# A longer warm-up and a new order of all instructions in a kernel of a long convolution and a gated MLP

## The chip, the cores and the metric

The kernel runs on one core of a Trainium2 chip. The metric is the device time of one execution in microseconds; lower is better. A core has five engines that run side by side, each through its own list of instructions in order: TensorE (PE, matrix multiplication), VectorE (DVE), ScalarE (ACT), GpSimd (POOL) and SyncE (SP). SP and ACT here also issue DMA transfers, each on a queue of its own. Engines wait for each other by semaphores only.

## What is computed

The reference, cut to what matters (x is A_q; S = 2048 positions, 512 channels, 1792 hidden units):

```python
xn = layernorm(x)
# long convolution
k_shift = sum(k_pad[:, t:t + S] * shift_k[:, 3 - t] for t in range(4))
kv = k_shift * v
y = irfft(rfft(kv, 2 * S) * rfft(ssm_k, 2 * S))[:S] + kv * ssm_D
s = xn * y
# gated MLP
h = gelu(xn @ w_gate) * (xn @ w_up)
g = silu(h @ w_down)
out = x + s * g
```

All inputs are bfloat16.

## The kernel before

The MLP is done in four quarters q of 512 positions. For a quarter, `ln` (L824) makes the statistics of its four tiles of x on VectorE (L827, L828, L835), a power on GpSimd (L836) and the normalized tile XN on VectorE or ScalarE (L845, L846). `xn_transpose` (L855) turns XN into xnT, for the first two quarters with TensorE transposes (L867) and an evacuation out of PSUM (L610 on ScalarE, L613 on VectorE), for the last two with a DMA transpose on SP's queue (L859). `unit` (L1130) is one of 14 blocks of 128 hidden units: four matmuls with w_gate and four with w_up (both recorded at L619), a GELU on ScalarE (L1149, L1158) and a product on VectorE (L1151, L1161). The first two blocks of the first quarter are done in halves of 256 columns. `down` (L1164) multiplies with w_down. w_gate and w_up come in four chunks (wg0 to wg3, wu0 to wu3: two blocks, then four each), w_down in two (wd0, wd1).

The convolution is a Fourier transform in two stages. The filter ssm_k (tiles Hn, loads h0 to h3) is transposed on TensorE (`h_transpose`, L883, matmuls at L891, evacuated to HTr) and goes through the first stage (`stage1`, L916): matmuls of HTr with the Fourier matrices F0 and F1, an evacuation by ScalarE or VectorE, and a store of 512 KB to the scratch tensor ZH, which ScalarE issues on its own DMA queue. `kshift` (L961) makes the shifted product of k and v on VectorE, whose first stage (L925) is stored to ZK by SP. The second stages read BH and BK back (L1001, in tiles of 32 by 32), the spectra are multiplied, transformed back, stored to ZI, read as BI, and the last stage (L1231) gives y.

At the very front TensorE has nothing to do until x arrives. `warm_up` (L677) fills that time with N_WARM matmuls of zeros with 512 columns into a bank that nobody reads.

All loads are issued by SP in the order of ORDER (L26), one list item after the other. The order of all other instructions is written out by hand, in SEQ (L27): a list of task numbers, in which a task is a few instructions on one engine (a "b" behind the number picks the second engine that it may run on). `Sched.run` (L345) walks through the list, emits the tasks to their engines in that order, and picks the buffer and the PSUM bank of each by a plan of times. LAND (L52) gives the plan's landing times of the loads, in ns; TAKEN (L301) is what a store on ScalarE's queue adds there to a load still in flight that stands ahead of it in the list. These times enter the program only through the choice of buffers; the order of each engine is SEQ's.

Of the kernel before, what the change touches and what calls it, by code (L numbers as in the profile page):

```python
# [21 lines left out]
NB = 2  # L22
LN_EPS = 1e-5
TURN = 8192
N_WARM = 12
ORDER = "x00 h0 x01 w0 D0 h1 w1 x1 h2 h3 s0 k0 w2 k1 k2 w3 d0 d1 k3 v2 v3 v0 v1 x2 x3"  # L26
SEQ = (  # L27
    "0 16 17 18 19 20 21 22 23 24 25 26 27 28 29 30 31 32 33 34 35 36 37 38 39 40 41 42 43 44 45 2 10 7 3 11 67 8 4 5 6 1 68 76 65 77 66 9 73 12 78 "
    "87 74 75 71 72 48 86 82 83 49 91 90 341 69 70 79 80 84 349 81 135 13 50 343 350 51 89 93 342 88 92b 137 351 352 14 52 54 344 53 55 345 346 353 "
    "134 355 15 354 356 365 347 348 124 125 431 425 426 427 104 429 129 105 369 361 367 371 56 428 366 58b 432 430 363 130 368 60 62 362 364 64 61 63 "  # L30
    "370 372 57 433 59 109 111 110 357 138 136 112 131 132 139 140 141 359 358 360 385 133 381 383 106 107 382 377 113 434 435 142 143 436 439b 384 "
    "126 144 379 378 380 146 437b 127 387 128 386 388 373 440b 119 397 443 441 374 375 376 389 447 147 148 438b 444 448 399 401 403 445 120 398 400 "
    "402 391 442 393 121 395 122 99 390 394 404 149 150 114 396 392 446 453 100 116 461 151 152 115 117 118 145 101 154 463 96 462 102 123 497 455 "
    "108 153 103 499 415 155 94 416 95 97 464 498 156 98 417 418 419 465 467 217 157 500 158 466 405 218 219 485 178 487 468 225 220 226 227 228 159 "
    "406 162 420 46 407 408 213 160 457 170 409 421 214 47 454 163 215 216 459 221 222 223 224 422 486 161 85 164 410 233 488 411 165 473 234 235 475 "
    "171 173 412 413 456 236 229 166 172 230 231 167 168 458 460 501 449 503 451 169 502 504 232 241 474 414 477 423 424 242 243 476 237 622 624 478 "
    "469 618 489 479 480 244 625 525 238 239 471 179 180 619 620 621 623 626 181 470 450 452 491 481 483 472 529 174 175 176 627 628 490 492 493 629 "
    "632 630 482 633 484 494 631b 495 496 240 183 182 184 531 505 527 510 506 245 526 185 532 528 530 533 186 246 706 258 188 177 282 634 534 247 249 "
    "520 507 515 248 250 259 187 261b 535 269 260b 198 516 511 536 537b 508 509 540b 538b 539b 541 517 252 518 519 189 190 521 191 192 251 262 512 "
    "513 514 522 523 524 193 253 256 639 263 254 655 657 635 637 283 284 285b 641 640 656 709 270 272 647 651 255 271b 658 642 264 265 267b 636 638 "  # L40
    "648 293 330 306 649 650 199 550 652 653 273 274 200 654 201 268 586 257 588 574 552 576 276 275 194 195 196 575 587 589 202 203 551 553 577 687 "
    "689 277 280b 278 197 590 592 546 294 279 548 286 287 296 295 208 547 549 570 572 591 593 307 309 308 297 298 281 266 688 690 578 288 289 291 290 "
    "566 568 580 299 571 567 573 569 204 205 206 300 310 317 659 542 660 543 712 661 662 544 545 311 209 210 562 211 212 594 596 579 581 301 302 304b "
    "564 303 207 563 595 597 305 318 320 565 671 319b 558 321 323 560 554 556 312 673 313 559 561 555 315 582 314 331 332 333 322 584 663 316 583 557 "
    "643 645 292 672 324 325 598 585 326 327 683 328 329 599 334 335 685 336 674 684 339 340 667 337b 338 686 665 664 600 601 703 666 608 669 675 677 "
    "644 609 646 694 602 695 603 610 611 679 668 681 604 670 696 713 710 612 680 682 676 678 605 613 606 714 766 711 764 698 697 699 719b 700 607 715 "
    "716 717 768 614 732 701 615 616 702 721b 725 739 723 724 617 718 720 770 733 691 692 693 707 771 704 705 722 760 761 734 726 740 746 769 767 727 "
    "765 735 747 741 753 728 742 708 762 763 729 748 736 737 738 730 731 749 754 755 743 744 745 756 750 751 752 757 758 759 "
)
NF_BANKS = 4  # L50
ISSUE = 470.0
LAND = {"x0_0": 3000, "h0": 6000, "x0_1": 7200, "wg0": 8300, "wu0": 9300, "D": 6500, "h1": 10700, "wg1": 12900, "wu1": 14600, "x1": 16000, "h2": 17400, "h3": 18700, "sk": 20000, "kh1": 21100, "kh113": 21300, "kz": 14000, "k0": 22700, "wg2": 24400, "wu2": 26100, "k1": 27600, "k2": 29100, "wg3": 30600, "wu3": 32100, "wd0": 34600, "wd1": 37200, "k3": 38500, "v2": 39800, "v3": 41100, "v0": 42400, "v1": 43700}  # L52
W_XT, W_SW, W_BK, W_BH, W_ZI, W_BI, W_ZK, W_MI, W_G1 = 1665000, 600000, 555000, 703000, 333000, 640000, 490000, 740000, 222000
NC_PAIRS = 4
SMALL = 1.15 * 262144
# [24 lines left out]
class Trk:  # L80
# [29 lines left out]
    def res(self, name, ap):  # L110
        t = ap.tensor
        tn = type(t).__name__
        if tn.startswith("SB"):
            key = "SB"
            addr = self.nc.lookup_mloc(t).addr
        else:
            assert tn.startswith("PS")
            key = "PS:" + t.name
            addr = 0
        esz = mybir.dt.size(ap.dtype)  # L120
        pairs = [list(q) for q in ap.ap]
        pst, pn = pairs[0]
        pstart = ap.offset // pst if pst else 0
        inner = ap.offset - pstart * pst
        hi = sum(st * (n - 1) for st, n in pairs[1:])
        r = Res(name, key, pstart, pstart + pn, addr + inner * esz, addr + (inner + hi + 1) * esz)
        lst = self.res_by_key.setdefault(key, [])
        for o in lst:
            if o.plo < r.phi and r.plo < o.phi and o.blo < r.bhi and r.blo < o.bhi:
                o.ovl.append(r)  # L130
                r.ovl.append(o)
        lst.append(r)
        return r
# [156 lines left out]
class Sched:  # L290
# [7 lines left out]
    SHARE_BW = 300.0  # L298
    FIRST = {"loads": 300.0, "SP": 37000.0}
    DRAIN, DRAIN2 = 121.0, 97.0  # L300
    SHARED, WAIT, TAKEN = 46000.0, 3300.0, 1400.0  # L301

    def __init__(self):
        self.tasks = []
# [91 lines left out]
def build_kernel(nc, A_q, A_k, A_v, A_shift_k, A_ssm_k, A_ssm_D, B_w_gate, B_w_up, B_w_down, out):  # L396
    with ExitStack() as es0:
# [11 lines left out]
        def new(name, shape, dt):  # L409
            h = at(name, shape, dt, place["at"])  # L410
            place["at"] += size(shape, dt)
            return h
# [4 lines left out]
        X = new("X", [128, NT, DM], BF16)  # L417
# [80 lines left out]
        S = Sched()  # L498
        res = trk.res

        def dsem(name):
            return DSem(nc.alloc_semaphore(name), name)
# [4 lines left out]
        def bank(b):  # L507
            return PSALL[:, 512 * b.slot:512 * (b.slot + 1)]
# [4 lines left out]
        def R_bank(b):  # L513
            return [R_ps[b.slot // 2][b.slot % 2]]
        R_X = [res(f"X{t}", X[:, t, :]) for t in range(NT)]
# [75 lines left out]
        def dma(eng, out_ap, in_ap, sem, r, w):  # L591
            trk.dma(eng, lambda e: e.dma_start(out=out_ap, in_=in_ap), sem, r=r, w=w)
# [3 lines left out]
        def load(name, out_ap, in_ap, w_res, w_buf, nbytes, ring="SP", r=(), rb=()):  # L596
            sem = dsem("d_" + name)
            last_load[0] = S.add([("loads", ISSUE)], lambda e: dma(ring, out_ap, in_ap, sem, r, w_res), r=rb, w=w_buf, nbytes=nbytes, land=float(LAND[name]))

# [18 lines left out]
        def mm(h, o, l, r, st, sp):  # L618
            return h.matmul(o, lhsT=l, rhs=r, start=st, stop=sp)  # L619
# [3 lines left out]
        bX = [[B(f"X{q}_{t}") for t in range(4)] for q in range(NQ)]  # L623
# [47 lines left out]
        bwarm = B("warm")  # L671
# [4 lines left out]
        warm = B("pswarm", pF)  # L676

        def warm_up(e):
            for i in range(N_WARM):
                trk.op("PE", lambda h: mm(h, bank(warm), ZERO[:, 0:128], ZERO, True, True), r=[R_zero], w=R_bank(warm), accum=True)  # L680

        t_warm = S.add([("PE", 10 * 390.0 + (N_WARM - 10) * 220.0)], warm_up, r=[bwarm], w=[warm])
        bcq, bck, bid32 = B("cq"), B("ck"), B("id32")
        S.add([("POOL", 420.0)], lambda e: pool_q(), w=[bcq])
        S.add([("POOL", 1000.0)], lambda e: pool_k(), w=[bck])
# [65 lines left out]
        x_dr = A_q[0].rearrange("(p t) d -> p t d", t=NT)  # L751
# [24 lines left out]
            x_late.append(S.add([("SP", ISSUE)], lambda e: dma(e, args[0], args[1], sem, [], args[2]), w=args[3], nbytes=480000, after=last_load))  # L776

        def load_x0(t):
            ts = slice(2 * t, 2 * t + 2)
            load(f"x0_{t}", X[:, ts, :], x_dr[:, ts, :], R_X[ts], bX[0][ts], 262144)  # L780

        def load_w(i, rings=("SP", "SP")):
            f0, n = FC[i]
# [117 lines left out]
        for k in range(KD):  # L901
# [4 lines left out]
                    r=[bHD, *[bHTr[k][0] for k in range(KD)]], w=[bFold], rr=[R_D, *R_HTr[0]], ww=R_HTr[0])  # L906
# [328 lines left out]
        for j in range(8):  # L1235
            p = p_y[j]
            ts = slice(2 * j, 2 * j + 2)
# [16 lines left out]
        for j in range(6):  # L1254
# [7 lines left out]
                  r=[b2], w=[B(f"out{j}")], nbytes=262144)  # L1262
# [55 lines left out]
```

## Time and profile before

| what | value |
| --- | --- |
| median of 3 runs | 194.51 us (194.4 to 194.63) |
| the profiled execution | 196.12 us, of it 194.3 us span |
| TensorE busy | 188.0 us, 1514 matmuls |
| VectorE busy | 158.2 us, 231 instructions |
| ScalarE busy | 137.7 us, 186 instructions |
| HBM | 27.39 MB read, 14.68 MB written |
| mean granted clock of TensorE | 0.991 |

The span runs from the program's first to its last instruction. "Busy" is the time in which an engine has at least one instruction of its own in flight; matmuls overlap, and their ends are modelled. A group of instructions is named by its line and by what it writes and reads (psall is the whole of PSUM). The chain of waits is followed back from the last instruction: at each step to what released it, or to the instruction before it on its engine. The granted clock is the share of its full clock at which TensorE was allowed to run.

### The profile page before, as it was taken

What the parts mean: (1) busy time and instruction counts of PE and PEld (TensorE: products, weight loads), DVE (VectorE), ACT (ScalarE), POOL (GpSimd) and SP (SyncE); (2) the same over time, 40 slices, a digit from 0 to 9 for tenths busy, and PEclk for the clock granted to TensorE, in tenths of its full rate; (3) what the DMA queues carried; (4) which work ended last, traced back from release to release, by engine and by line L of the source; (5) the groups of instructions that cost most, each with busy time, mean ns of one, the idle gap of its engine ahead of it and who ended that gap; (6) DMA issues with size and microseconds to landing.
All of it is one profiled execution on the core that took longest, in us unless ns stands there. A gap on an engine that the chain in (4) does not pass through costs nothing.

```text
span 194.3 us, 3771 instructions
## 1 busy us (share of the span) xinstructions
PE 188.0 (97%) x1514; PEld 84.7 (44%) x1514; DVE 158.2 (81%) x231; ACT 137.7 (71%) x186; POOL 14.3 (7%) x32
## 2 busy tenths in 40 slices
PE   7699999999999999999999999999999999999993
PEld 2485644544434333343434433343444354444452
DVE  4878799989999798977897898899788762279784
ACT  2787899698687889895969487878767643263452
POOL 5311360000000000023000000000000000000000
PEclk9789999999999999999999999999999999999999
DMA  5999999993967997589999997841353344866056
GB/s 154 353 384 346 364 365 370 411 401 117 363 204 246 303 270 200 199 287 320 273 285 180 335 369 266 281 140 54 126 201 108 110 163 131 305 216 216 22 200 213
DMA packets 36423, 47.86 MB, mean 246 GB/s; under 512 B 7347, under 2 KB 26039, under 8 KB 36406
## 3 DMA queue, kind: packets, MB, share of 16 engines
q1 hardware_dynamic: 29878, 39.23, 62.6%
q10 hardware_dynamic: 6528, 8.39, 12.2%
q8 instruction: 12, 0.20, 0.4%
q14 instruction: 5, 0.04, 0.1%
HBM read 27.39 MB, written 14.68 MB: 217 GB/s over the span
## 4 chain that ended last, share of the span: by engine, by line
PE 94%; DMA 2%; DVE 2%; ACT 0%; issue 0%
PE psall L619 80%; PE psall L1001 6%; PE psall L891 2%; PE psall L925 2%; DMA X<-in_A_q_dram 2%; PE psall L1231 2%; PE psall L867 1%; DVE stats L827 1%; DVE G L1196 0%; DVE G L1195 0%; ACT G L1193 0%; DVE XN L846 0%; DVE mv L835 0%; DVE mv L828 0%; DVE C L701 0%
## 5 line engine op out<-in xcount | busy, mean ns | idle before, releaser
L619 PE MATMUL psall<-xnT,Wg 128*128 128x512 bf16 (+1 forms) x232 | 56.3, 376 | 0.0
L619 PE MATMUL psall<-xnT,Wu 128*128 128x512 bf16 (+1 forms) x232 | 55.7, 372 | 0.0
L619 PE MATMUL psall<-Wd,HT 128*128 128x512 bf16 (+2 forms) x238 | 52.3, 367 | 0.0
L1161 DVE TENSOR_TENSOR HT<-psall,GE 128x512 bf16<-128x512 f32 x54 | 36.5, 687 | 18.8 <-PE psall L619 17.5
L1158 ACT ACTIVATE GE<-psall 128x512 bf16<-128x512 f32 x54 | 31.3, 600 | 9.1 <-PE psall L619 8.1
L619 PEld LDWEIGHTS psall<-Wd,HT 128*128 128x128 bf16 x238 | 21.9, 98 | 27.1 <-issue 3.8
L619 PEld LDWEIGHTS psall<-xnT,Wg 128*128 128x128 bf16 x232 | 22.0, 99 | 25.9 <-issue 2.2
L619 PEld LDWEIGHTS psall<-xnT,Wu 128*128 128x128 bf16 x232 | 21.4, 98 | 25.7 <-issue 2.6
L610 ACT ACTIVATE BO<-psall 128x1024 bf16<-128x1024 f32 x18 | 17.9, 1022 | 12.0 <-PE psall L1231 6.5
L1104 DVE TENSOR_TENSOR HSW<-KB,HSW 128x2048 bf16<-128x2048 bf16 x16 | 19.1, 1218 | 1.8 <-ACT KB L610 1.7
L610 ACT ACTIVATE HSW<-psall 128x1024 bf16<-128x1024 f32 x16 | 15.5, 1026 | 2.8 <-PE psall L1001 2.8
L1185 ACT ACTIVATE G<-psall 128x512 bf16<-128x512 f32 x12 | 7.2, 596 | 12.4 <-PE psall L619 12.4
L984 DVE TENSOR_TENSOR KAC<-KAC,KTM 128x2048 bf16<-128x2048 bf16 x12 | 14.6, 1220 | 0.2
L982 DVE TENSOR_TENSOR KTM<-KK,SKB 128x2048 bf16<-128x2048 bf16 x12 | 14.6, 1219 | 0.1
L610 ACT ACTIVATE KB<-psall 128x1024 bf16<-128x1024 f32 x11 | 10.8, 1022 | 4.3 <-PE psall L1001 4.3
L610 ACT ACTIVATE AST<-psall 128x1024 bf16<-128x1024 f32 x12 | 12.2, 1020 | 1.1 <-PE psall L925 0.7
L836 POOL TENSOR_TENSOR mv<-mv,NHALF 128x1 f32<-128x1 f32 (+1 forms) x7 | 6.8, 970 | 69.2 <-DVE mv L835 69.2
L827 DVE BATCH_NORM_STATS2 stats<-X 128x6 f32<-128x512 bf16 x16 | 10.4, 678 | 1.7 <-DMA X<-in_A_q_dram 1.7
L1104 DVE TENSOR_TENSOR KB<-KB,HSW 128x2048 bf16<-128x2048 bf16 x8 | 9.7, 1218 | 0.0
L610 ACT ACTIVATE XN<-psall 128x1024 bf16<-128x1024 f32 x8 | 8.1, 1020 | 1.5 <-PE psall L619 1.3
L619 PE MATMUL psall<-HTr,F 128*128 128x512 bf16 x32 | 8.7, 379 | 0.0
L613 DVE CAST BO<-psall 128x1024 bf16<-128x1024 f32 x5 | 6.1, 1223 | 2.6 <-PE psall L1001 2.6
(83 smaller groups left out, 162.3 us busy)
## 6 DMA issues: line engine op xcount, KB each, us to landing
BH<-ZH SPq DMA_DIRECT2D x8, 512.0 KB, 5.0
HSW<-HSW SPq DMA_DIRECT2D x16, 256.0 KB, 2.8
BK<-ZK SPq DMA_DIRECT2D x8, 512.0 KB, 6.0
ZI<-BO ACTq DMA_DIRECT2D x16, 256.0 KB, 3.4
BI<-ZI SPq DMA_DIRECT2D x8, 512.0 KB, 4.6
ZK<-AST SPq DMA_DIRECT2D x6, 512.0 KB, 3.2
Hn<-in_A_ssm_k_dram SPq DMA_DIRECT2D x4, 512.0 KB, 7.4
KK<-in_A_k_dram SPq DMA_DIRECT2D x4, 512.0 KB, 12.0
```

The lines of the kernel that those rows point to most:

```text
L610: return h.activation(o, i, ACTF.Copy, scale=scale)
L613: return h.tensor_copy(o, i)
L619: return h.matmul(o, lhsT=l, rhs=r, start=st, stop=sp)
L827: t_stats[t] = op([("DVE", 670.0)], lambda e, h, t=t: h.bn_stats(stats[:, t, :], X[:, t, :]), r=[bX[q][t % 4]], w=[bst[t]], rr=[R_X[t]], w ...
L836: t_pw = op([("POOL", 850.0 if q else 600.0)], lambda e, hd, ts=ts, n=n: hd.tensor_tensor(mv[:, ts, 3:4], mv[:, ts, 2:3], NHALF[:, 0:n, :] ...
L982: op([("DVE", dur)], lambda e, h, j=j, m=m: h.tensor_tensor(KTM[:, m.slot, :, :], kk(j), sk(j), ALU.mult), r=need + [bSKB[j], a], w=[m], r ...
L984: op([("DVE", dur)], lambda e, h, m=m: h.tensor_tensor(KAC[:, a.slot, :, :], KAC[:, a.slot, :, :], KTM[:, m.slot, :, :], ALU.add), r=[m], ...
L1001: trk.op("PE", lambda h: h.matmul(ps(s, i)[b, :], lhsT=wt(col)[a, :], rhs=data(col)[a, :], start=n < 16, stop=n >= len(todo) - 16, tile_po ...
L1104: return hd.tensor_tensor(pair(KB, *(2 * DM * z for z in slots())) if to else x, k, x, ALU.mult)
L1158: op([("ACT", act(512))], lambda e, h: h.activation(GE[:, g.slot, :], bank(pg), ACTF.Gelu_apprx_tanh), r=[pg], w=[g], rr=lambda: R_bank(pg ...
L1161: op([("DVE", dve(512, 1))], lambda e, h: h.tensor_tensor(HT[:, q % 2, m, :], bank(pu), GE[:, g.slot, :], ALU.mult), r=[pu, g], w=[bHT[q][m]],
L1185: op([("ACT", act(n))], lambda e, h, g=g, pc=pc: h.activation(g, pc(), ACTF.Tanh, scale=0.5), r=[p], w=[bt], rr=lambda p=p: R_bank(p), ww= ...
```

## The change

Six constants change, one of them the order of everything.

```diff
-N_WARM = 12
+N_WARM = 19
 ORDER = "x00 h0 x01 w0 D0 h1 w1 x1 h2 h3 s0 k0 w2 k1 k2 w3 d0 d1 k3 v2 v3 v0 v1 x2 x3"
 SEQ = (
-    "0 16 17 18 19 20 21 22 23 24 25 26 27 28 29 30 31 32 33 34 35 36 37 38 39 40 41 42 43 44 45 2 10 7 3 11 67 8 4 5 6 1 68 76 65 77 66 9 73 12 78 "
+    "0 3 2 10 1 11 7 8 9 16 67 65 68 66 17 18 19 76 4 5 12 73 6 48 49 51 71 77 78 87 74 75 20 72 82 21 86 22 91 83 90b 349 341 52 50 69 70 79 23 351 "
...
-LAND = {"x0_0": 3000, "h0": 6000, "x0_1": 7200, "wg0": 8300, "wu0": 9300, "D": 6500, "h1": 10700,
+LAND = {"x0_0": 4900, "h0": 6100, "x0_1": 6900, "wg0": 7800, "wu0": 8700, "D": 6000, "h1": 10000,
...
-    SHARED, WAIT, TAKEN = 46000.0, 3300.0, 1400.0
+    SHARED, WAIT, TAKEN = 46000.0, 3300.0, 1600.0
...
-        t_warm = S.add([("PE", 10 * 390.0 + (N_WARM - 10) * 220.0)], warm_up, r=[bwarm], w=[warm])
+        t_warm = S.add([("PE", 7 * 427.0 + (N_WARM - 7) * 217.0)], warm_up, r=[bwarm], w=[warm])
```

The rest of LAND, all in ns, before and after: wg1 12900 and 11500, wu1 14600 and 13000, wg2 24400 and 22600, wu2 26100 and 25000, wg3 30600 and 29200, wu3 32100 and 30500, wd0 34600 and 32700, wd1 37200 and 34900, v1 43700 and 41200, and the others alike. `load_x0` (L778) is written differently and issues the same two loads.

What SEQ's new list does to the engines:

- SP: the loads keep their order. Behind them come the three small DMA transposes (G1 and the two of MI), then ZK stores, the late loads x2 and x3, and the first two BH loads, which were first, third and so on before. The later BH, BK, HSW and xnT entries change places by a few. Two of the small outputs, which stood behind all large ones, now stand between them.
- TensorE: behind the warm-up come eight transposes of Hn (h0), then eight of XN, then the first eight gate matmuls; before, the transposes of XN and Hn alternated, four at a time. 72 matmuls of 512 columns (without the warm-up) stand ahead of the first one that reads wu3, where 94 did, and 64 ahead of the first that reads wg3, where 78 did. The first one that reads wd0 has 138 ahead of it, where 142 did.
- ScalarE: the first evacuation of h stands ahead of the first of xnT. The first two ZH stores stand directly behind each other, after the GELU of the first block that uses wg2; the next two follow singly.
- VectorE: the phase tables and the sine arguments come first, then both statistics of the first two tiles, both aggregates and both additions of eps, the statistics of the third tile, and then the first two XN.
- GpSimd: the four index tables ARR and OFF stand ahead of Q and K4.

## What I predict

> **What bounds the kernel now.** I read the busy shares first, then the waits of TensorE, then the chain that ended last, then the granted clock by stretches, and last the DMA traffic around 30 us.
>
> ```profile
> PE 188.0 (97%) x1514; PEld 84.7 (44%) x1514; DVE 158.2 (81%) x231; ACT 137.7 (71%) x186; POOL 14.3 (7%) x32
> ```
> ```profile
> PE psall L867 <- DVE XN L846: 1.9, 1, 1.9
> PE psall L619 <- DVE Q L704: 1.2, 1, 1.2
> ```
>
> TensorE is the bound, and it waits only twice: 1.2 us until the zeros for the warm-up are there, and 1.9 us between the warm-up and the first normalized tile of x.
>
> ```profile
> 4.86 0.69 DVE stats L827
> ...
> 7.35 0.40 PE psall L867 x4
> 7.74 0.89 PE psall L891 x4
> ...
> 37.30 2.59 PE psall L619 x12
> ...
> 182.55 8.02 PE psall L619 x43
> 190.59 0.50 ACT G L1193
> ```
>
> From 7.35 to 190.59 us the chain is one unbroken row of TensorE pieces (those between are left out), so a microsecond saved or lost on TensorE anywhere there is one of the whole kernel. The prices at full clock: a 512-column matmul 2.59/12 = 0.216 us, a 256-column one 0.11, a transpose of Hn (L891) 0.11, one of XN (L867) 0.055.
>
> ```profile
> 0.87:4.28 3.41, 3.07 (x8) 1.00 0.57 153
> 4.28:7.70 3.42, 1.54 (x11) 1.00 1.05 348
> 7.70:11.11 3.41, 3.41 (x20) 0.50 1.06 361
> 11.11:14.53 3.42, 3.42 (x37) 1.00 1.06 399
> 188.60:192.02 3.42, 2.51 (x24) 1.00 0.91 328
> ```
>
> Columns: stretch, its length, TensorE busy (instructions), granted clock, DMA share, GB/s; I cut the stretches where the clock changes, every 3.41 us. A stretch with TensorE busy for 1.54 of 3.42 us (45%) was followed by one at half clock. The stretch from 188.60, with 2.51 (73%), was not. The mark lies somewhere between.
>
> ```profile
> 18.06 2.28 SPq L592 DMA_DIRECT2D Wu<-in_B_w_up_dram  x1
> ```
> ```profile
> Wu<-in_B_w_up_dram SPq DMA_DIRECT2D x1, 512.0 KB, 12.9
> ```
> ```profile
> 27.66 0.40 ACTq L592 DMA_DIRECT2D ZH<-X  x1
> 28.90 0.37 ACTq L592 DMA_DIRECT2D ZH<-X  x1
> ```
> ```profile
> DMA packets 1169, 1.71 MB, mean 398 GB/s; under 512 B 42, under 2 KB 646, under 8 KB 1169
> ## 3 DMA queue, kind: packets, MB, share of 16 engines
> q10 hardware_dynamic: 544, 1.05, 63.6%
> q1 hardware_dynamic: 625, 0.66, 43.5%
> ```
>
> The last chunk of w_up (wu3) is issued at 18.06 and lands 12.9 us later, at 31.0. The first two stores of ZH go out on ACT's queue (q10) at 27.66 and 28.90. The last fence is 31.7 to 36.0: the stores move 1.05 MB there and the loads (q1) only 0.66 MB, 153 GB/s. From 29.0 to 31.7 q1 moved its bytes alone at 349 GB/s. So a store takes effect 4.0 us after its issue and then takes over half of the DMA from the loads. Before, TensorE comes to wu3 at 38.0, seven microseconds after the landing.
>
> **The change part by part.** *Seven more dummies.* 7 x 0.216 = 1.5 us. They run from 5.3 to 6.8, in the 1.9 us in which TensorE waits anyway, and no work is ready sooner (h0 lands at 6.1 and is transposed next). Cost 0; with no cover it would be 1.5. What they buy is the clock: the stretch 4.28 to 7.70 is now filled, so that 7.70 to 11.11 runs at full.
>
> *The front.* The eight transposes of h0 now come first, 0.88 us, to 7.7. DVE does both statistics of x0_0, both aggregates and both additions of eps before any XN, and has the statistics of x0_1 in front of XN, which wait for that load (6.9). POOL's power takes 0.58 us. XN 0 and 1 end at about 7.9 and 8.25 (before 7.3 and 8.2), their transposes at 8.2 and 8.5, and ACT, which moves an h block first (1.02 us), has their xnT (0.6 us) at about 9.4. The first eight gate matmuls start at about 9.47, against 9.75. Lead 0.28 us. From 9.75 to 11.11 the kernel before runs at half clock and loses 1.36/2 = 0.68 us; the new one doesn't if the clock holds. It has gaps of 0.14, 0.1 and some 0.8 us after 7.7, so is busy for some 70%, next to the 73% that held. Gain **0.96 us**; bounds 0.6 to 1.3 (xnT as late as before with the clock held; h not in front of it on ACT), and -0.75 where the clock is lost (below).
>
> *POOL's index tables in another order, the sine tables earlier.* DVE's first L704 waits for POOL's fifth operation, about 2.1 us instead of 1.06; all of it stands under the warm-up and the first load (4.84). Cost 0; without that cover 1.1.
>
> *The new order to 32 us.* Loads are issued in the same order, none behind a new wait, so land as before, until the stores interfere. TensorE's position when it first needs wu3 is counted from the new order. After 9.47 come 32 matmuls of 256 columns, 24 L891, 8 L867 and 72 of 512: 3.52 + 2.64 + 0.44 + 15.55 = 22.15, so 31.6 us. Before, 94 of 512 columns, more transposes and the cold front stood ahead: 38.0. The new order moves the third and fourth chunks of w_gate and w_up forward by six microseconds. The first ZH store stands behind a GELU whose matmul is the 40th of 512 columns: 9.47 + 3.52 + 2.64 + 0.44 + 8.64 = 24.7, its evacuation starts at 24.9, and the store goes 0.15 later as before: 25.05, with the second right behind it. That is 2.6 us sooner than 27.66. Their bytes then flow from 29.1. Ahead of wu3's landing are then the last 0.3 us of wg3 (0.1 MB) and its own 0.52 MB: 0.63 MB at 153 GB/s = 4.1 us, 33.2. TensorE waits 33.2 - 31.6 = **1.6 us**. Behind that matmul in the queue stands everything else of TensorE. Bounds: 0 (the stores slip by a microsecond, or take effect later) and 1.8 (all their bytes ahead, 33.4). I take 1.6, the row of the same kind of store against the same kind of load. What is late next is wd0, but TensorE needs that after 66 more matmuls and some transposes, 15 us on.
>
> The Trainium skill's DMA: Bandwidth & Descriptors (Queues, rings and completion order) says that each DMA engine takes turns between the queues a packet at a time. The trace agrees: 544 packets of the stores, 1.9 KB each, against 625 of the loads, 1.1 KB each.
>
> *The order from 32 us on.* The groups in which TensorE changes its tile shape are as many as before: 8 of L925, 4 of L1231, and 24 of L1001 in the same sizes, so 0 there. On SP's queue the three small transposes now come right after the loads and the first BH load behind three stores; SP issued that load at 54.99, and the first matmul that reads BH comes at 81. Both xnT transposes (DVE and DMA work alike around them) keep their places among the BK loads within a few entries. I take 0; bounds -0.3 and +1.3, one 512 KB load late by the 1.3 us between two landings. The list ends with the same instructions after TensorE's last matmul.
>
> *Sum:* -0.96 + 1.6 = +0.64 us. The profiled execution has a span of 194.3 in 196.12 us; the runs' median is 194.51, 1.6 below that execution, so I carry the difference only: 194.51 + 0.64 = **195.2 us**.
>
> **The rivals.** *The weights are on time* (the other side): the stores of ZH take effect after 31.0, and TensorE never waits for wu3. Then -0.96: 193.55 us. If the stores' bytes flow from x, wu3 lands at x + (31.0 - x) x 349/153, which is 31.6 for x = 30.5, a store issue of 26.5: from there on the wait is gone. For it: a slip of 1.4 us, or stores that take effect that much later, suffices. Against it: the stores hang on TensorE's own progress, and the trace shows 4.0 us.
>
> *The wait costs the clock.* 1.6 us idle, all of it in the stretch 31.59 to 35.00, leaves about 53% busy, between the 45% that lost the clock and the 73% that kept it. A stretch at half clock loses 3.41/2 = 1.7: 194.51 + 0.64 + 1.7 = 196.9 us. The Trainium skill's TensorE: Matmul & The Clock Gate (Why this matters for your kernels) allows gaps up to about 3 us. By that the clock holds and 195.2 stands; the half-clock stretch after the gap of 1.9 us speaks against it.
>
> *The front loses the clock.* If 70% is too little, 11.11 to 14.53 runs at half: -0.96 + 1.7 = +0.75. All stores come 1.7 us later and the wait for wu3 vanishes: 195.3 us.
>
> *The clock never was the matter.* The timed runs lie 1.6 us under the profiled one, about one cold stretch; if they had none, only the lead of 0.28 is left and the stores come early all the same; or the order and the wait even out: 194.2 to 194.8 us.
>
> **How the numbers follow.** The forecast 0.36, weights on time 0.24, wait and clock 0.20, clock lost in front 0.10, no matter 0.10. 0.2% is 0.39 us, about what these runs can tell from no change. Slower: 0.31 of the forecast's 0.36 (a wait under 1.35 us gives no change), 0.20, 0.09 and nothing of the last: 0.60. Faster: 0.24, and 0.03 of the last: 0.27. No change: 0.13. The range from 193.4 (weights on time, the best front) to 197.0 (wait and clock) leaves out a later stall on top of these. The likeliest case's own range is 194.4 to 195.8.
>
> **What would show it.** The granted clock 1.00 from 7.70 to 11.11; the first gate matmul near 9.5; the stores' issues near 25.05; TensorE idle before a group xnT,Wu near 31.6 with wu3 landing near 33. It is wrong if TensorE's waits name another releaser after 12 us, or if the store's bytes appear later than 4 us after the issue.

## The result and the profile after

The changed kernel takes 197.5 us (median of 4 runs, 196.52 to 198.62) against 194.57 before: ratio 1.0154, 95% interval 1.012 to 1.0189. It is 1.5% slower, 0.5 us above the predicted range. The profiled execution is a quick one: 196.52 us, span 194.7. As before, 1.82 us lie around the span. Medians below are over all executions of a run; the ratios leave out those more than 1.5% above the run's fastest, one each in a2, b2 and e2 and two in d1.

The engines' busy times and TensorE's waits of the changed kernel, and its clock in the stretches that were shown of before (length, TensorE busy and instructions, granted clock, DMA share, GB/s):

```profile
PE 188.7 (97%) x1521; PEld 84.3 (43%) x1521; DVE 160.7 (83%) x236; ACT 134.1 (69%) x181; POOL 14.3 (7%) x32
```

```profile
PE psall L619 <- DVE stats L827: 1.2, 1, 1.2
PE psall L619 <- DVE G L1187: 0.4, 1, 0.4
```

```profile
0.87:4.28 3.41, 3.08 (x8) 1.00 0.71 174
4.28:7.70 3.42, 3.42 (x15) 1.00 1.03 334
7.70:11.11 3.41, 2.21 (x25) 1.00 1.06 364
11.11:14.53 3.42, 3.42 (x32) 1.00 1.06 401
```

The cold stretch is gone, as forecast, and the stretch with 65% busy (2.21 of 3.41) kept the clock (70%, if it is cut where this execution's clock steps, from 9.24 to 12.66). But TensorE has a new wait of 1.2 us ahead of the first gate matmul. The chain of waits says what sets the time (start, us, what):

```profile
1.20 6.54 PE psall L619 x19
7.75 0.88 PE psall L891 x8
8.62 0.46 PE psall L867 x8
...
9.11 0.42 DVE xnT L613
9.53 0.61 DVE stats L827
```

```profile
32.49 13.05 DMA V<-in_A_v_dram
...
46.71 1.22 DVE KTM L982
47.93 0.60 DVE HT L1161
48.53 1.13 DVE KAC L978
...
60.18 0.61 DVE G L1187
60.79 0.05 issue
60.83 3.63 PE psall L619 x16
```

Before, the chain was one row of TensorE pieces. Now it runs from 45.54, where the first quarter of V lands, over fifteen microseconds of VectorE work without a gap, to a G that TensorE waits for at 60.83. Up to there TensorE is not the bound in this execution: what it does earlier, it waits for later. By the prediction's own sign (another releaser than wu3 after 12 us) the forecast was wrong here: the wait is for G (L1187).

### The profile page after: what moved, and what is told of

It reads as the page before. It is cut to its first block, busy times and chain, and to the rows that moved or that the text cites. A ratio compares the mean times of both kernels' runs of the same rounds, so it can differ in the third digit from the quotient of the medians.

```text
span 194.7 us, 3787 instructions
## 1 busy us (share of the span) xinstructions
PE 188.7 (97%) x1521; PEld 84.3 (43%) x1521; DVE 160.7 (83%) x236; ACT 134.1 (69%) x181; POOL 14.3 (7%) x32
## 3 DMA queue, kind: packets, MB, share of 16 engines
q10 hardware_dynamic: 6528, 8.39, 12.0%
## 4 chain that ended last, share of the span: by engine, by line
PE 71%; SPq 11%; DVE 9%; DMA 7%; issue 1%; ACT 0%; DVEq 0%
PE psall L619 60%; SPq L592 11%; DMA V<-in_A_v_dram 7%; PE psall L1001 6%; DVE KTM L982 2%; PE psall L1231 2%; DVE KAC L984 2%; PE psall L925 1%; DVE KAC L978 1%; DVE HT L1161 1%; DVE V L986 1%; PE psall L891 0%; DVE stats L827 0%; DVE G L1187 0%; DVE G L1196 0%
## 5 line engine op out<-in xcount | busy, mean ns | idle before, releaser
L619 PE MATMUL psall<-xnT,Wg 128*128 128x512 bf16 (+1 forms) x232 | 54.7, 372 | 1.2 <-DVE stats L827 1.2
L619 PE MATMUL psall<-Wd,HT 128*128 128x512 bf16 (+2 forms) x238 | 53.1, 367 | 0.0
L1158 ACT ACTIVATE GE<-psall 128x512 bf16<-128x512 f32 x54 | 31.8, 599 | 13.1 <-PE psall L619 10.4
L619 PEld LDWEIGHTS psall<-xnT,Wg 128*128 128x128 bf16 x232 | 21.7, 98 | 27.4 <-issue 2.6
L610 ACT ACTIVATE BO<-psall 128x1024 bf16<-128x1024 f32 x18 | 17.8, 1022 | 13.6 <-PE psall L1001 8.6
L610 ACT ACTIVATE HSW<-psall 128x1024 bf16<-128x1024 f32 x16 | 15.5, 1021 | 5.2 <-PE psall L1001 5.2
L1187 DVE SCALAR_TENSOR_TENSOR G<-G,psall 128x512 bf16<-128x512 bf16 x12 | 8.2, 682 | 6.1 <-ACT G L1185 6.1
L610 ACT ACTIVATE AST<-psall 128x1024 bf16<-128x1024 f32 x9 | 9.2, 1026 | 1.9 <-PE psall L925 1.7
L836 POOL TENSOR_TENSOR mv<-mv,NHALF 128x1 f32<-128x1 f32 (+1 forms) x7 | 5.4, 777 | 69.6 <-DVE mv L835 69.6
L610 ACT ACTIVATE X<-psall 128x1024 bf16<-128x1024 f32 x8 | 8.1, 1029 | 1.7 <-PE psall L619 1.7
## 6 DMA issues: line engine op xcount, KB each, us to landing
KK<-in_A_k_dram SPq DMA_DIRECT2D x4, 512.0 KB, 12.6
```

The source lines that it names most:

```text
L610: return h.activation(o, i, ACTF.Copy, scale=scale)
L1158: op([("ACT", act(512))], lambda e, h: h.activation(GE[:, g.slot, :], bank(pg), ACTF.Gelu_apprx_tanh), r=[pg], w=[g], rr=lambda: R_bank(pg ...
L1187: op([("DVE", dve(512, 1))], lambda e, h, g=g, pc=pc: h.scalar_tensor_tensor(out=g, in0=g, scalar=1.0, in1=pc(), op0=ALU.add, op1=ALU.mult ...
```

## The experiments

Below, "start to start" means the distance between the starts of two matmuls beyond the 0.216 us that one of 512 columns takes (0.11 for 256); it shows waits that a row of the profile gives some 0.2 us shorter. All ratios are to runs of the kernel before on the same chip, whose median was 194.38 to 194.61 in the five groups.

### The two kernels again, and the dummies apart from the order

```diff
 a1: no edit to the kernel before; a2: none to the changed one
 a3, in the kernel before (N_WARM and with it the plan of times stay):
-            for i in range(N_WARM):
+            for i in range(19):
 a4, in the changed kernel (likewise):
-            for i in range(N_WARM):
+            for i in range(12):
```

> The kernel before, unchanged, to see how far its profiled span moves by itself. Theory W (the warm-up's length and the clock's phase set the front): the moment of the full clock moves by up to 3.4 us from execution to execution, and the span lies between about 192.6 us (no cold stretch after the warm-up) and 194.3 us. Theory O (the order sets the loss): the span is within 0.4 us of 194.3 again.

> The changed kernel, unchanged. Theory W: its span spreads over 194.5 to 197 us with the moment of the full clock (full clock 1 us later costs 0.5 us more of warm-up). Theory O: the spread comes from waits behind 20 us, and the warm-up ends within 0.3 us of 7.6 us.

> The order before with 19 dummies. Theory W: 1 to 2.5 us slower than before, because dummies that run cold end at 7.6 us or later, behind the first normalized tile at 7.3. Theory O: within 0.4 us of before, or faster by the cold stretch that the dummies prevent (up to 1.7 us).

> The new order with 12 dummies. Theory W: 1 us or more faster than the changed kernel, to within 1 us of before. Theory O: within 0.4 us of the changed kernel (197.5 us).

| run | median us | ratio, 95% | first XN transpose | first Wg matmul | last G of VectorE |
| --- | --- | --- | --- | --- | --- |
| before, a1 | 194.43 | 0.9998 | 6.66 | 8.62 | 190.38 |
| before, 19 dummies, a3 | 195.32 | 1.0041 (1.0025 to 1.0057) | 8.23 | 10.03 | 191.66 |
| changed, 12 dummies, a4 | 196.87 | 1.0116 (1.0097 to 1.0136) | 7.93 | 9.16 | 192.27 |
| changed, a2 | 197.38 | 1.0141 (1.0115 to 1.0168) | 7.88 | 9.70 | 192.82 |
| changed, profile after | 197.5 | 1.0154 (1.012 to 1.0189) | 8.46 | 10.27 | 192.43 |

The dummies alone cost 0.9 us, the order alone 2.4, both 2.9. So dummies on top of the new order cost some 0.5 us, where the intervals of a4 and a2 still overlap. And the execution of before that the prediction was worked on was not a usual one. This is a1, TensorE's waits and the same stretches:

```profile
PE psall L867 <- DVE XN L846: 1.3, 1, 1.3
PE psall L619 <- ACT xnT L610: 0.2, 1, 0.2
```

```profile
4.28:7.70 3.42, 2.16 (x17) 1.00 1.02 319
7.70:11.11 3.41, 3.22 (x33) 1.00 1.07 367
```

The first gate matmul starts at 8.62 in place of 9.75, and no stretch is cold: there was no clock to win back. The timed executions say how rare the other kind is. Of 89 of the kernel before in the five groups, three have a mean granted clock of 0.991, as the one that the prediction was worked on, and take 196.02 to 196.09 us; the other 86 have 0.997 or more and take 194.2 to 195.31.

### Which stretch of the order loses

```diff
 in the kernel with 12 dummies, SEQ:
 (LAND and TAKEN: b1 and b3 those of before, b2 and b4 the new ones)
 b1: the new list to "92b" (14 us), the rest from the list before
 b2: the list before to "92b", the rest from the new one
 b3: the new list to "169" (some 70 us), the rest from the list before
 b4: the list before to "168", the rest from the new one
```

> 12 dummies; the new order of all engines as far as the xnT copy of tile 2 (about 14 us), the old order from there. Leaves nothing out. Of the 2.4 us that the new order cost with 12 dummies (196.87 against 194.44), theory F puts about half into this stretch: in the new order DVE takes the stats of x0_1, which wait for that load, before the two XN, and ACT takes the HTr copy before the xnT copy, so that TensorE waits for XN and for xnT (1.27 and 0.52 us in the run with 12 dummies, against 1.3 and 0.2 at an earlier place in the run of before). F: 195.0 to 195.7. Theory M (all of it is lost between 14 and 65 us): 194.2 to 194.6. Theory F-all (all of it is in front): 196.5 to 197.1.

> The mirror image, 12 dummies: the old order of all engines as far as the xnT copy of tile 2, the new order from there. F: the other half, 195.5 to 196.2. M: 196.5 to 197.1. F-all: 194.2 to 194.6. If an earlier front is given back by the middle (the loads of V and the k-shift decide there, whatever the front does), b1 and b2 don't add up: b2 stays at 196.5 or more, and b1 lies at 195 too.

> 12 dummies; the new order as far as the last k-shift of DVE (about 65 to 70 us), the old order from there. If nothing of the loss lies behind 65 us (F, M and F-all alike): 196.5 to 197.1. Theory L (the late part, with its small TensorE waits at 93 to 187 us, costs 0.5 us or more): below 196.4.

> The mirror image of b3, 12 dummies: the old order as far as about 70 us, the new order from there. F, M and F-all: 194.2 to 194.7. Theory L: 195.0 or more.

b1 195.31 (ratio 1.0033, 1.0017 to 1.0049), b2 197.21 (1.0137, 1.0103 to 1.0171), b3 198.16 (1.0185, 1.0153 to 1.0216), b4 194.43 (0.999, 0.9969 to 1.001). b4 says that nothing of the loss lies behind 70 us. b3 loses with the old constants and b4 doesn't with the new ones, so the loss goes with the list and not with LAND. The new front before the old rest costs 0.9 us; the old front before the new rest is no better than the whole new order (196.87). But joints cost too: b2's profile has a wait of 0.83 us at 12.6, b3's waits of 1.0 us at 75 to 78 and b1's one of 0.25 at 12.5 (start to start), which a1 and a4 don't have; b3 missed what was expected by about its joint. So most of the loss sits between 14 and 70 us, and whether an earlier front helps there, b2 alone can't say. b2's profile shows the wait that I had forecast: TensorE's waits, then its row beside the issues of the stores.

```profile
PE psall L619 <- DMA Wu<-in_B_w_up_dram: 1.6, 1, 1.6
PE psall L619 <- DMA Wg<-in_B_w_gate_dram: 0.7, 1, 0.7
```

```profile
31.86 1.03 PE L619 MATMUL psall<-xnT,Wu 128*128 128x512 bf16 x4
34.52 1.02 PE L619 MATMUL psall<-xnT,Wu 128*128 128x512 bf16 x4 [1.64 <-DMA Wu<-in_B_w_up_dram]
```

```profile
26.02 0.90 ACTq L592 DMA_DIRECT2D ZH<-X  x2
```

```profile
Wu<-in_B_w_up_dram SPq DMA_DIRECT2D x1, 512.0 KB, 16.0
```

wu3 is issued at 18.41 and takes 16.0 us to land, where it took 12.9 before. The two orders, by when each load is first used and when it landed (the DVE or TensorE instruction behind the wait for it):

| | k0 | wg2 | k1 | wg3 | wu3 | V0 |
| --- | --- | --- | --- | --- | --- | --- |
| before (a1): used at | 22.4 | 24.9 | 32.5 | 32.2 | 36.4 | 45.5 |
| landed at | 21.9 | 23.9 | 26.8 | 29.6 | 31.9 | 45.0 |
| changed, 12 dummies (a4): used at | 21.4 | 23.8 | 26.4 | 30.4 | 32.1 | 45.4 |
| landed at | 21.2 | 22.7 | 26.0 | 28.9 | 31.7 | 45.4 |

The old order uses k1 5.7 us and wu3 4.5 us after the landing, the new one 0.4 us. Over all profiles but d3 and d4, whose loads are held up, wg2 landed anywhere from 22.6 to 25.1, wu3 from 30.6 to 34.6, the latter in part for the stores (below). The new LAND has them at 22.6 and 30.5, about the earliest of these.

### Mending one place after the other

```diff
 in the changed kernel with 12 dummies, SEQ
 c1, the first two ZH stores (133, 108) later on ScalarE:
-383 133 377 36 108 111 ... 439b 112 367 366 ... 440b 117
+383 377 36 111 ... 439b 112 367 133 366 ... 440b 108 117
 c2, KV0 (145) behind two k-shift steps (151, 152) on VectorE:
-396 44 145 403 443 447 151 126 100 402 404 119 154 152 155
+396 44 403 443 447 151 126 100 402 404 152 145 119 154 155
 c3, the front: stats of x0_1 (71) behind the XN (78, 75), HTr (51) behind xnT (91):
-49 51 71 77 78 87 74 75 20 72 82 21 86 22 91 83 90b
+49 77 78 87 74 75 71 20 72 82 21 86 22 91 51 83 90b
 c4: all three
```

> The changed kernel with 12 dummies (196.87 in its own run); on ACT the issue of the two first ZH stores is moved some 2 to 4 instructions later (the first behind the GELU that follows at 28.8 us of the plan, the second behind the XN that follows at 30.0), nothing else. Leaves nothing out. Theory S (the two early stores take DMA from wu3, and TensorE waits for wu3 in many executions): both stores issued after 26.5 us, wu3 lands at about 31 instead of 31.7 to 34.4 us, 195.9 to 196.4. Theory J (all loads land when they do, and the new order uses each as soon as it can land: wu3, V0, k1 with no slack; the stores matter little): 196.6 to 197.1. A wait of ACT for the slots that the stores free later would show as a new TensorE wait at 33 to 38 us and 197 or more.

> The changed kernel with 12 dummies; on DVE the product with V0 (KV0, which waited for V0 until 45.4 to 45.9 us) is moved behind the two steps of the next k-shift and the HT product that follow it, so that DVE has about 3 us of work ahead of it that doesn't need V0. Leaves nothing out. Theory V (DVE's wait for V0 delays HT, G and the k-shift, which TensorE meets at 48.9, 58 and 61 us, 0.85 us in sum in one profile): 196.0 to 196.5. If DVE catches up anyway: 196.7 to 197.0.

> The changed kernel with 12 dummies; the stats of x0_1 go behind the two XN on DVE, and ACT's HTr copy behind its xnT copy, as in the kernel before; nothing else. Leaves nothing out. First Wg matmul at 8.4 to 8.7 us in place of 9.16. Theory F (what the front loses is lost at the end): 196.1 to 196.5. If the middle is bound by landings (J), the earlier front only waits longer for wg2, wu3 and V0, as the old front before the new rest did (197.21): 196.7 to 197.3.

> The edits of c1, c2 and c3 together. If S, V and F each hold and add up: 194.4 to 195.2. J: 196.3 to 197.2, since only later use of all loads, not of one, would give the slack back.

c1 196.89 (1.0125, 1.01 to 1.015), c2 196.93 (1.0118, 1.008 to 1.0155), c3 198.1 (1.0168, 1.0132 to 1.0204), c4 195.64 (1.0053, 1.0035 to 1.0072). One place alone gains nothing in the median, and the mended front alone is worse (three of its six executions lie at 198.6 to 198.7, the others at 196.8 to 197.6); all three together take 1.2 us off. The profiles still show the edits of c1 and c2 at work. First the stores:

| | stores 1 and 2 issued | wg3 landed | wu3 landed | behind wg3 | TensorE waits for wu3 |
| --- | --- | --- | --- | --- | --- |
| a4 | 24.9, 25.3 | 28.9 | 31.7 | 2.8 | 0 |
| after | 25.8, 26.2 | 29.0 | 30.7 | 1.7 | 0 |
| a2 | 25.2, 25.6 | 29.4 | 32.1 | 2.7 | 0.1 (start to start) |
| b2 | 26.0, 26.4 | 30.7 | 34.4 | 3.7 | 1.6 |
| b3 | 25.0, 25.4 | 29.5 | 33.3 | 3.8 | 0.8 |
| c2 | 26.2, 26.6 | 30.9 | 34.6 | 3.7 | 0.5 |
| c3 | 24.9, 25.3 | 29.2 | 32.6 | 3.4 | 0.4 |
| c1 | 28.4, 28.8 | 29.4 | 30.9 | 1.5 | 0 |
| c4 | 27.5, 27.9 | 29.7 | 31.2 | 1.5 | 0 |

Two loads land 1.5 us apart with the stores out of the way, and up to 3.8 with a pair of stores issued by 26.6. With the stores at 27.4 or later wu3 was on time in each of these profiles. c1 alone would not show the cause, since a4, from which it was made, has no wait for wu3 either; the column "behind wg3" does. KV0 is the product of the shifted k with the first quarter of V. Its row in c4, to be read against the chain above: VectorE still waits 1.0 us for V0, but with two steps less behind it, and TensorE has no wait at 59 to 62.

```profile
47.02 1.22 DVE L986 TENSOR_TENSOR V<-KAC,V 128x2048 bf16<-128x2048 bf16 x1 [1.04 <-DMA V<-in_A_v_dram]
```

```profile
59.30 0.61 PE L925 MATMUL psall<-V,F 64*128 64x512 bf16 x4
59.84 1.90 PE L619 MATMUL psall<-xnT,Wu 128*128 128x512 bf16 x8
```

TensorE's instructions stand in the same order in a4 and c1 to c4, so each can be compared one by one. Between 56 and 61 us c2 and c4 both make up 0.72 us on a4; c1 makes up 0.28, c3 nothing to speak of. What c3 gained ahead of 9 us (0.4 at the XN transposes) was gone at 9.4: one xnT copy was left on VectorE behind the statistics. c2's profiled execution had its loads some 2 us later than a4's (wg2 at 25.1 against 22.7, k1 at 27.9 against 26.0) and waited for wg2 (1.0 us), for XN (1.1) and for wu3 (0.7, all start to start), which ate c2's gain.

One place was still open, the XN wait. Here is ScalarE in the changed kernel, and GpSimd in a4:

```profile
28.12 0.81 ACT L845 ACTIVATE XN<-X,NB__69,mv 128x512 bf16<-128x512 bf16 x1 [1.78 <-POOL NB__69 L841]
```

```profile
24.22 1.02 POOL L836 TENSOR_TENSOR mv<-mv,NHALF 128x4 f32<-128x4 f32 x1 [2.38 <-DVE mv L835]
25.32 1.20 POOL L840 TENSOR_TENSOR NB__69<-mv 128x4 f32<-128x4 f32 x1
26.60 1.09 POOL L841 TENSOR_SCALAR NB__69<-NB__69 128x4 f32<-128x4 f32 x1
```

ScalarE stands still for 1.8 us for GpSimd's NB (the bias of the normalization), GpSimd has waited 2.4 us for VectorE's eps (L835), and VectorE has that 0.16 us instruction behind the k-shift steps that wait for k0. Behind ScalarE's XN stands an evacuation that frees TensorE's bank: 0.48 us, start to start, at 29.5 in a4.

### The middle mended, and later loads for both

```diff
 d1, d2: the edits of c1 and c2, and eps of x1 (433) ahead of the k-shift
-428 64 29 30 ... 138 139 433 434
+428 64 433 29 30 ... 138 139 434
 d1: 12 dummies, the list before to "92b", then this; d2: 19 dummies, the new front
 d3, in the kernel before, and d4, in the changed one with 12 dummies (load):
-lambda e: dma(ring, out_ap, in_ap, sem, r, w_res)
+lambda e: [dma(ring, out_ap, in_ap, sem, r, w_res) for _ in range(1 + (name == "sk"))]
```

> 12 dummies; the old order as far as 14 us, then the new order with three edits in the middle: the first two ZH stores issued some instructions later and KV0 behind two steps of the next k-shift (both as before), and DVE's eps of x1 (0.16 us) ahead of the k-shift step that waits for k0 (ACT waited 2.2 us for the NB that follows from it, and TensorE 0.48 us for ACT, at 29.5 us). Leaves nothing out. Against the old front before the new rest (197.21), theory J' (the middle's loss is three places that use or wait for a load with no slack - k0 and eps, wu3 and the stores, V0 - and nothing else): 194.4 to 194.9. If each place mended only moves the wait to the next landing: 195.8 to 197.2.

> The changed kernel with its 19 dummies and its own front, with the same three edits in the middle. Leaves nothing out. J': what stays is the front's loss alone, 1.1 to 1.65 us by the profiles (first Wg at 9.70 to 10.27 in place of 8.62): 195.5 to 196.2. If the front's loss was given back by the middle's waits, the mended middle gains little: 196.8 to 197.4.

> The kernel before, with the 512 KB load of the taps (sk) issued twice, so that every load behind it (k0 to v1) lands some 1.4 us later; the second copy writes the same values. J' (the old order uses its loads with slack: k1 5.4 us, wu3 1 us or more, V0 0.5 us): 194.8 to 195.6, 0.3 to 1.1 more, V0's share; all of the 1.4 us if its loads had no slack: 195.8.

> The changed kernel with 12 dummies and the same doubled load. J' (no slack at k0, k1, wu3, V0): 198.0 to 198.6, 1.1 to 1.7 more than the 196.87 without it. If its loss were in the front alone or in the late part: as much more as the kernel before shows, or less.

d2 196.13 (1.0077, 1.0051 to 1.0102; 195.73 to 196.26), as expected: three edits in the middle take 1.3 us of the changed kernel's 2.9 off, and its runs lie within 0.5 us of each other where they had spread over 2. Its only wait that is left of those of the changed kernel is the front's 1.2 us. In its profile the first gate matmul starts at 10.43, 1.8 us behind a1's, and VectorE's last G comes 1.7 us behind (192.05): what is left of the loss is the front. d1 missed: 196.05 (1.0064, 1.0041 to 1.0087), with runs from 195.2 on. TensorE has no wait in its profile between 25 and 60 us, but one of 0.9 for ScalarE's HTr copy at 12.8, where the old front's last copies meet the new order's early use of them: a cost of the joint, as in b2, not of either list.

d3 and d4 missed too: 197.52 (1.0149) and 201.67 (1.0363). The second copy of the taps waited for the first and held SP's queue, so k0 landed at 25.5 and 26.0 and wg2 at 27.0 and 27.5, three to five microseconds later and not 1.4. No order had that much in hand at wg2. That the changed kernel lost 4.8 and the one before 3.1 fits, but tells little of k1, wu3 and V0, which it was meant to test. Part of the difference is the clock: four of d4's six executions have a mean granted clock of 0.982 to 0.991, two of d3's have 0.991. What the two show is that clock; here are d3 and, for comparison, b2, cut where each one's clock steps:

```profile
23.68:27.09 3.41, 1.07 (x5) 1.00 1.03 344
27.09:30.51 3.42, 3.38 (x9) 0.50 1.04 395
```

```profile
32.83:36.24 3.41, 1.77 (x12) 1.00 1.08 398
36.24:39.65 3.41, 3.41 (x20) 1.00 1.06 408
```

In d3 a wait of 2.4 us leaves a stretch 31% busy, and the next runs at half clock; in b2 a wait of 1.6 us leaves 52%, and the clock stays. The two executions of d3 at 0.991 took 198.36 and 198.48 us, the other four 196.81 to 197.52.

### Front and middle

```diff
 12 dummies, the edits of c1, c2 and eps; e2 is this alone, e1 has in front:
-49 51 71 77 78 87 74 75 20 72 82 21 86 22 91 83 90b
+49 77 78 87 74 75 71 20 72 82 21 86 22 91 90 51 83
```

> The new order with 12 dummies, the three edits of the middle as in d2, and a front mended further than in c3: the stats of x0_1 behind the two XN on DVE, both xnT copies on ACT ahead of both HTr copies (c3 had left one xnT copy on DVE behind those stats, and TensorE waited 1.1 us for it). Leaves nothing out. J': no place of loss is left but 0.2 us at h2, and the late part costs nothing: 194.4 to 194.9, the time of the kernel before. If something else is slow in the new order: 195.2 or more.

> The same without the edits of the front: 12 dummies, the new front, the three edits of the middle. Leaves nothing out. J': the front's 0.54 us of the profile with 12 dummies is what remains, 194.9 to 195.4; against d2 (196.13) the difference, 0.7 to 1.2, is what the seven dummies cost in the new order.

e2 195.39 (1.0042, 1.0025 to 1.0058), the upper end of what was expected; the seven dummies cost 0.7 in this order (d2 against e2). e1 missed: 195.52 (1.0053, 1.003 to 1.0075). Its first gate matmul came at 8.77, 0.4 us ahead of e2's, and TensorE gave it back one by one, start to start: 0.2 at h1 (9.8), 0.1 at 13.6, 0.3 at 21.1, 0.25 at 29.4. These waits are on h1's landing and on VectorE and ScalarE; which edit would free them was not tried. No version here beats the kernel before; b4 equals it.

## Why the prediction was wrong

The forecast was +0.64 us and +2.9 came, because its two terms and its zero each failed, and so did its base. The front was a loss of 1.65 us (profile after) and 1.08 (a2) against a usual execution of before, in place of a gain of 0.96; the wait for wu3 was 0 and 0.1, in place of 1.6; and the order from 32 us on, put at 0, cost 0.5 in the profile after, behind VectorE's KV0, and 1.1 in a2, with all waits between 48 and 61.5 us.

*The account.* In the profiles, a1 against a4 (the new order alone): first gate matmul 0.54 later, 0.16 more for h2 at 15.5, 0.48 for XN at 29.5, and 0.72 between 56 and 61, which is what moving KV0 takes away. Sum 1.90, less 0.12 for a wait of a1's own at 10.7; VectorE's last G came 1.89 later. The changed kernel itself, the profile after against a1: first gate matmul 1.65 later and 0.49 more at 60.83, less the 0.12; the last G came 2.05 later. In a2 it is 1.08 in front, 0.3 at 29.5 and 32.2, and 1.1 between 48 and 61.5; the last G came 2.44 later. The profile after starts 1.1 us behind a4 and ends 0.16 behind, for it meets no wait for h2 or XN and a shorter one at KV0's place: a part of the late front is won back there. The medians differ by 2.4: the profiled a4 was one of the quicker executions (196.36), without a wait for wu3. That the rest is wu3 and late loads is what b2, b3, c2 and c3 suggest; for the unprofiled runs it is not shown.

*"Seven more dummies. Cost 0."* Wrong: 0.9 us in the old order, some 0.5 to 0.7 in the new. I priced each at 0.216 and let them end at 6.8. They start 0.43 us apart and come 0.216 apart only once the clock has risen, which was at 5.83 in the profile after and anywhere from 3.95 to 7.13 in five profiles (after, a1 to a4); nineteen ended at 7.17 to 8.39. And the cover of 1.9 us was that of one execution. In a1 the first transpose of XN runs at 6.66, in a3, behind the dummies, at 8.23: 1.6 us later.

*"The front: -0.96."* Wrong in sign. Its 0.68 for the cold stretch was a loss that usual executions of before don't have, and its base, a gate matmul at 9.75, is 8.62 in a1. The new front itself came at 10.27 and 9.70 where I had 9.47; the wait before it was 1.2 where I had some 0.8. So the term was a loss of 1.65 and 1.08 us against a1. That the clock is held at some 70% busy was right (70% in the profile after).

*The sum, carried as a difference onto the median.* This step failed most. I saw that the profiled execution lay 1.6 us above the median, about one cold stretch, and gave the rival that says so 0.10. With its base the front would have been a loss in my own steps: 9.47 against 8.62 is +0.85, and with the 1.6 for wu3 the sum is 197.0. That is near the result, but by luck: its 1.6 for wu3 isn't in the changed kernel's two profiles, and what stands there in its place, the larger loss in front and KV0, isn't in the sum.

*"TensorE waits 1.6 us for wu3."* The mechanism is there, but the term was wrong for the changed kernel: the wait was 0 and 0.1 us in its two profiles. In the profile after the stores went out at 25.75 (I had 25.05), their bytes appear at 29.66, 3.9 us behind the issue, and over the next 4.0 us the loads move 0.57 MB, 143 GB/s, where they moved 349 just before; I had 4.0 us and 153. But only the tail of wu3 was left by then: it landed at 30.7, where I had 33.2. TensorE came to it at 32.1 to 32.5 in after, a2 and a4 (31.6). In the variants the wait, start to start, went up to 1.8, in b2, whose wu3 landed at 34.4. That early stores make wu3 late is shown by the gap behind wg3; that they cost time in the unprofiled executions of the changed kernel is not.

*"The order from 32 us on: 0, bounds -0.3 and +1.3."* Wrong by 0.7 in a4 and 0.5 in the profile after. I looked at SP's queue and the tile shapes, not at VectorE, where KV0 now stands ahead of work that TensorE needs. V0 lands at 45.4 to 45.9 (a4, after, a2), 0.4 to 0.9 us later than in a1; what counts is what is queued behind the wait, for c4 has V0 at 47.0 and no such wait of TensorE. The wait for XN at 29.5 was not in the prediction at all.

*The sine tables* cost nothing that shows. *The late part* (from 70 us) was rightly 0: b4.

*The rivals.* "The wait costs the clock" didn't come in any profile: b2's 1.6 us left a stretch 52% busy, and the next kept the clock. (One of the ten timed executions of the changed kernel, a2's 199.77 us, has a mean clock of 0.991, about what one half-clock stretch gives; it has no trace, so its cause is open.) The twenty profiles, each cut where its own clock steps, narrow the mark down: stretches busy for 5% (d4), 31% (d3) and 45% (before) lost the clock, those with 49% (b3, from 191.3), 52% (b2), 63% (a1) and more kept it. So here the mark lies between 45% and 49% of a stretch of 3.41 us, busy as the profile models it. The Trainium skill's TensorE: Matmul & The Clock Gate (Why this matters for your kernels) lets TensorE idle for up to about 3 us; d3 lost the clock with less, as did the profiled execution of before with 1.9, and the measurement decides.

## What to carry to other kernels

Before working on a profile, compare its time to the median: one that lies a clock stretch above it has waits and covers that usual runs don't have. An order planned with the landings of one trace uses each load the moment it landed there, and every later landing becomes a wait; keep the slack at least as wide as the landings scatter (2.5 us for wg2 here, 4 for wu3 with the stores), above all on a queue whose head waits for a load while others need what stands behind it. Where several such places lie in a row, an edit to one of them can move only the wait to the next, so mend them together before saying that a place costs nothing.

## What was not expected of the hardware

The clock's first rise came anywhere from 3.95 to 7.22 us into the span in the twenty profiles, with the same start of the warm-up (1.2 us), so a number of dummies doesn't fix when they end. Counted back in steps of 3.41 us from each rise, the rise ends the first stretch of which the warm-up, running without a gap, filled 80% or more (a4: from 0.54 to 3.95); where it filled 76% (d4: from 0.40 to 3.81), the clock rose only one stretch later, at 7.22. The Trainium skill's TensorE: Matmul & The Clock Gate (What's actually happening) has the reason in a window of 3413 ns that runs freely; the half-clock stretches of before and d3, 3.41 us long, agree, and the scatter of 3.3 us is about one such window. The page speaks of 0.5 us either way, though also of 6, 11 or 14 cold matmuls in runs of one kernel; here 7 started cold in a4 and 14 in a3. GpSimd's power over four columns (L836) took 1.02 us in a4 and 3.06 us in a1; spans on GpSimd are rough in these profiles, and no run here tells why.
